# Between attention and experts: earlier stores, gathers ahead of expert numbers, second expert's weights loaded in advance

## The chip, the cores and the metric

The program runs on one core of a Trainium2 chip. The metric is the time of one execution on the device, in microseconds (us). A core has five engines that each work through their own instructions in order: TensorE (PE, with its weight loads listed apart as PEld), VectorE (DVE), ScalarE (ACT), GpSimd (POOL) and SyncE (SP). In this kernel SP issues nearly all plain DMAs, and POOL issues the indirect ones (gathers and scatters of rows by index). Engines wait for each other, and for DMAs, through semaphores.

## The reference

Attention over 2 x 576 rows with 8 heads, then a mixture of 8 experts with one expert per row, then a dense two-layer block. Cut to what matters:

```
x = attention(q, k, v)                  # rotary q and k; softmax; 1152 rows of 512
logits = normalised(x) @ normalised(expert_emb).T / tau
expert_idx = argmax(logits, axis=1)
for e in range(8):                      # w1[e]: 512 x 1024, w2[e]: 1024 x 512
    mask = expert_idx == e
    h = maximum(x[mask] @ w1[e], 0)
    out[mask] = gate_w[mask, None] * (h @ w2[e])
g = softplus(out @ w_in)                # 512 x 2048
result = g @ w_out                      # 2048 x 512
```

For the inputs that are timed, the reference sends 109, 200, 97, 486, 143, 31, 85 and 1 rows to the eight experts.

## The kernel before, in words

All matrix products are in float32, made of parts: each operand is split into a high part (a cast on ACT) and the rest (a subtraction on VectorE), and three products are added up. The program is written out in order by hand (`tc.manual_schedule()`): each engine gets its instructions in the order in which the Python code records them, and the tile framework adds the semaphore waits.

Three stages follow each other. **Attention** handles 16 heads in a loop over 72 steps; `xout` (L629 to L637) turns the output of a head into `xrow`, the rows of x, with one VectorE instruction per head (L637) and into `zp`, its share of the expert logits (L636). `x_store` (L170, L171) writes columns of `xrow` to `xs` in DRAM, where the rows can be gathered by expert. The columns of heads 8 to 13 (batch 1, `0:6*D`) are stored from inside the loop.

The **transition** decides which row goes where. `first_max` finds the expert of each row, `rank_mm`, `count_mm`, `places` and `at_places` number the rows within their experts by small matmuls, and `sequence` and `block_places` lay them out in blocks of at most 128 rows of one expert: at most 16 blocks, here 13. `idx[:, n]` holds the rows of block n, `eid[n]` its expert, `chg[n]` whether the expert differs from that of block n - 1. `gather(n)` (L963) fetches block n from `xs` into one of three buffers `xg`. PE runs `warm(WARM1)` (L676), 40 small matmuls whose results are not used.

The **expert stage** then goes through the blocks: `x_t` transposes the gathered rows (PE, L968), `x_ev` splits them (ACT L972, VectorE L973), `layer1` (L989), `relu` (L996), `h_t` and `h_ev` (again L968, L972, L973), `layer2` (L1018). Weights come in quarters of 512 KB: `fetch_w(n, l, c)` loads quarter c of layer l for block n into `raws_w[l, c]` (`raw00` to `raw03` for layer 1, `raw10` to `raw13` for layer 2), `split_hi` casts it on ACT (L950), `split_lo` subtracts on VectorE (L954) and then asks for the same quarter of the next block. For a block whose expert is that of the block before, the load is skipped by a condition in the DMA. Expert 0's first-layer weights are loaded and split during attention and lie elsewhere (`first_weights`), so that `raw00` to `raw03` are first written for block 1. A final stage does the dense block.

Around the change the order on SP is: the store of columns `0:6*D` (L170, L171), four loads of expert 0's second layer (L939), the store of the last two heads' columns (L170, L171), then, once `eid` can be read into registers (L943), the four loads of block 1's first layer (L945). Each SP DMA takes the next of eight completion semaphores in turn and waits until that semaphore's last DMA has landed; in the listings they are DMAHW0 to DMAHW7.

Of the kernel before, what the change touches and what calls it, by code (L numbers as in the profile page):

```python
# [20 lines left out]
ALU = mybir.AluOpType  # L21
# [74 lines left out]
def moe_kernel(ctx: ExitStack, tc: tile.TileContext, q, k, v, emb, tau, w1, w2, w_in, w_out, rope, tab, out):  # L96
# [182 lines left out]
    def sequence(cnt, q):  # L279

        used = w([P, E, E], "used")
        V.tensor_tensor(used, bc(cnt, E, 2), bc(tb("thr"), E, 1), op=ALU.is_gt)
        nov = q["nov"] = w([P, E], "nov")
        V.tensor_reduce(nov, used, axis=AX.X, op=ALU.add)
        yield
        V.tensor_tensor(used, tb("lt").rearrange("p (a b) -> p a b", a=E), bc(nov, E, 1), op=ALU.mult)
        st = q["st"] = w([P, E], "st")
        V.tensor_reduce(st, used, axis=AX.X, op=ALU.add)
        V.tensor_tensor(st, st, tb("ev"), op=ALU.add)
        be = q["be"] = w([P, NBLK, E], "be")  # L290
        V.tensor_tensor(be, bc(tb("n16"), E, 2), bc(st, NBLK, 1), op=ALU.is_ge)
        ef = w([P, NBLK], "ef")
        V.tensor_reduce(ef, be, axis=AX.X, op=ALU.add)
        V.tensor_scalar(eid, ef, -1.0, None, op0=ALU.add)
        V.tensor_tensor(chg[:, 1:NBLK], ef[:, 1:NBLK], ef[:, 0:NBLK - 1], op=ALU.not_equal)

    def block_places(q):
# [3 lines left out]
        V.tensor_tensor(total, nov[:, E - 1:E], st[:, E - 1:E], op=ALU.add)  # L301
        V.tensor_scalar(nblk, total, 1.0, None, op0=ALU.add)
        ok, at = (w([P, JB, E], n) for n in ("ok", "at"))
# [38 lines left out]
    with actx:  # L342
# [173 lines left out]
        heads, tiles = {}, {}  # L516
        late, rest = [], []

# [105 lines left out]
        def xout(i, left=None):  # L624
# [7 lines left out]
            def ev():  # L632
                ri = heads[i]['ri']
                V.reciprocal(ri, ri)
                ri = ri.unsqueeze(2)
                V.tensor_tensor(zp[b][:, :, h], px[:, :, D:D + E], ri.to_broadcast([P, 5, E]), op=ALU.mult)  # L636
                (rest if i == NH - 1 else late).append(lambda: V.tensor_tensor(xrow[b][:, :, h * D:h * D + D], px[:, :, 0:D], ri.to_broadcast([P, 5, D]), op=ALU.mult))  # L637

# [275 lines left out]
    if True:  # L914
# [15 lines left out]
        def fetch_w(n, l, c):  # L930

            if n >= NB:
                return
# [4 lines left out]
            if n == 0:  # L938
                SY.dma_start(raws_w[l, c], src[0, c])  # L939
                return  # L940
            always = n == 1 and l == 0
            if n not in regs:
                regs[n] = [SY.value_load(t[0:1, n:n + 1], min_val=0, max_val=m) for t, m in ((eid, E - 1), (chg, 1))]  # L943
            e, new = regs[n]
            SY.dma_start(raws_w[l, c], src[ds(e, 1), c].rearrange("e p f -> (e p) f"), **({} if always else dict(cond=new > 0)))  # L945

# [196 lines left out]

        for c in range(4):
            fetch_w(0, 1, c)
        pr1, pval, pcnt = bank(5), bank(JB), bank(1)[:, 0]
# [6 lines left out]
        for _ in first_max(1):  # L1153
            pass
        for r in rest:
            r()
        x_store(1, 6 * D, DM)
        rank_mm(1, pr1)
        count_mm(1, pcnt)
        for c in range(4):  # L1160
            split_hi((0, 1, c))
# [9 lines left out]
        gather(0)  # L1171
        V.tensor_copy(vals[0], pval)
        for _ in sgen:
            pass
        for c in range(4):
            fetch_w(1, 0, c)
        block_places(q)
        in_block(q, 1, 5)
        V.tensor_scalar(idx[:, 1:5], choose(q, vals[0], 1, 5)(), float(SKIP), None, op0=ALU.add)
        gather(1)  # L1180
        gg = [gate(b, gate_tmp) for b in range(B)]
        for _ in range(2):
            next(gg[0])
        split_lo((0, 1, 0))
        x_ev(0, x_t(0))
        for _ in layer1(0):
            pass
# [9 lines left out]
        for _ in range(4):  # L1197
            next(gg[0])
        for c in range(1, 4):
            split_lo((0, 1, c))  # L1200
        in_block(q, 5, NBLK)
# [254 lines left out]
```

## Time and profile before

| what | us |
|---|---|
| median of 3 runs (593.17 to 597.6) | 593.63 |
| profiled execution | 594.01 |
| its span, first to last instruction | 592.2 |
| PE busy | 549.3 |
| VectorE busy | 464.9 |
| ACT busy | 438.2 |

In a timeline a row gives start, duration, engine, line, operation, output and inputs, the number of merged instructions and, in brackets, how long the engine was idle before it and what ended that. A windows row gives, for a stretch, its length, then each engine's busy time with instructions in parentheses, then the clock that PE was granted as a share of 2.4 GHz (0.50 is 1.2 GHz), the mean busy share of the 16 DMA engines and what they moved. Names lose their buffer numbers in the profile: `raw` stands for all eight weight quarters.

### The profile page before, as it was taken

To read this page: it belongs to the slowest core of one execution; us is meant where nothing else is said; L and a number is where in the kernel's file an instruction comes from. 1 tells how busy PE (TensorE), PEld (TensorE's weight loads), DVE (VectorE), ACT (ScalarE), POOL (GpSimd) and SP (SyncE) were. 2 spreads that over 40 slices of the span, in tenths; PEclk is the share of its full clock that TensorE was granted. 3 is DMA by queue.
4 is the path that set the end of the run, shared out by engine and by line. 5 is a ranking of instruction groups with operands and counts; after the bars stand their busy time and mean duration, and the time that the engine had idled before them with its cause. 6 is when DMAs were issued, how large, how long until landed. Compare 5 with 4: busy or idle time off the path is not lost. (4 is left out here: it accounts for less than half of the span.)

```text
span 592.2 us, 9785 instructions
## 1 busy us (share of the span) xinstructions
PE 549.3 (93%) x3227; PEld 479.0 (81%) x3227; DVE 464.9 (79%) x775; ACT 438.2 (74%) x827; POOL 202.9 (34%) x305
## 2 busy tenths in 40 slices
PE   5699999999997789999999999969999999999995
PEld 4489999999986668787777888858888999888994
DVE  7998787879787499989999998776877766687233
ACT  3678878887875287599998898777877877767551
POOL 7999998569422330132222261200000000000033
PEclk9899999999998689999999999998999999999998
DMA  5423000061006635594348696262232222100012
GB/s 152 125 70 96 23 1 3 28 193 61 7 1 222 233 126 169 203 343 156 119 147 308 257 378 228 87 221 91 88 107 85 94 71 72 37 0 1 1 72 89
DMA packets 37270, 70.56 MB, mean 119 GB/s; under 512 B 8146, under 2 KB 23890, under 8 KB 37088
## 3 DMA queue, kind: packets, MB, share of 16 engines
q1 hardware_dynamic: 34272, 62.64, 31.8%
q0 software_dynamic: 2800, 7.09, 3.3%
q8 instruction: 27, 0.44, 0.3%
q10 hardware_dynamic: 144, 0.16, 0.2%
q14 instruction: 27, 0.22, 0.1%
HBM read 89.01 MB, written 8.13 MB: 164 GB/s over the span
## 5 line engine op out<-in xcount | busy, mean ns | idle before, releaser
L954 DVE TENSOR_TENSOR wt<-raw,wt 128x1024 fp32r<-128x1024 f32 x100 | 116.4, 1220 | 5.7 <-ACT wt L950 5.7
L1319 PE MATMUL ph<-yt,wt 128*128 128x320 f32 (+1 forms) x576 | 106.9, 340 | 4.2 <-ACT r__5678 L1331 3.4
L1319 PEld LDWEIGHTS ph<-yt,wt 128*128 128x128 f32 x576 | 95.1, 191 | 13.5 <-ACT r__5678 L1331 3.8
L1366 PE MATMUL po<-wt,g 128*128 128x512 f32 x432 | 104.0, 391 | 0.7 <-ACT g L1350 0.5
L950 ACT CAST wt<-raw 128x1024 fp32r<-128x1024 f32 x100 | 98.9, 1068 | 3.5 <-DMA raw<-in_moe_w_dram 1.9
L1366 PEld LDWEIGHTS po<-wt,g 128*128 128x128 f32 x432 | 80.2, 188 | 18.0 <-ACT g L1350 1.0
L1018 PE MATMUL py<-wt,ht 128*128 128x512 f32 x312 | 76.7, 397 | 3.3 <-DVE wt L954 2.6
L1383 POOL DMA_INDIRECT out_dram<-acc,otok x9 | 9.6, 1066 | 191.1 <-DVE acc L1380 190.5
L989 PE MATMUL ph<-wt,xt 128*128 128x512 f32 x288 | 71.0, 401 | 3.6 <-ACT hr L996 3.1
L1018 PEld LDWEIGHTS py<-wt,ht 128*128 128x128 f32 x312 | 57.5, 188 | 17.1 <-DVE wt L954 4.5
L989 PEld LDWEIGHTS ph<-wt,xt 128*128 128x128 f32 x288 | 54.2, 192 | 15.1 <-ACT hr L996 3.3
L562 ACT ACTIVATE p<-sc,nm 128x576 f32<-128x576 f32 x72 | 53.9, 749 | 15.4 <-DVE nm L556 15.4
L556 DVE TENSOR_REDUCE nm<-sc 128x1 f32<-128x576 f32 x72 | 54.1, 752 | 2.3 <-PE sc L552 1.3
L575 ACT CAST ph<-tp 128x512 fp32r<-128x512 f32 (+1 forms) x80 | 42.8, 546 | 14.8 <-PE tp L568 14.4
L552 PE MATMUL sc<-kt,qt 128*128 128x288 f32 x256 | 50.2, 318 | 2.1 <-ACT p L562 1.2
L586 DVE TENSOR_TENSOR pl<-tp,ph 128x512 fp32r<-128x512 f32 (+1 forms) x80 | 49.4, 627 | 0.0
L568 PE MATMUL tp<-idf,p 128*128 128x128 f32 x288 | 44.7, 278 | 4.8 <-DVE pl L586 3.5
L402 POOL TENSOR_TENSOR t<-qk,ropet 128x256 f32<-128x256 f32 x58 | 41.6, 745 | 10.9 <-DMA qk<-in_k_dram 10.5
L1351 DVE TENSOR_TENSOR g<-e,g 128x512 fp32r<-128x512 f32 (+2 forms) x33 | 24.3, 740 | 25.3 <-ACT g L1350 25.3
L1350 ACT CAST g<-e 128x512 fp32r<-128x512 f32 (+2 forms) x33 | 21.7, 659 | 30.3 <-PE po L1366 22.9
L613 PE MATMUL po<-ph,vs 128*128 128x288 f32 x128 | 36.5, 307 | 3.7 <-DVE kt L456 1.4
L568 PEld LDWEIGHTS tp<-idf,p 128*128 128x128 f32 x288 | 32.3, 144 | 9.0 <-issue 4.2
(246 smaller groups left out, 1023.2 us busy)
## 6 DMA issues: line engine op xcount, KB each, us to landing
raw<-in_moe_w_dram SPq DMA_DIRECT2D x112, 512.0 KB
raw<-in_moe_w_in_dram SPq DMA_DIRECT2D x16, 512.0 KB
raw<-in_moe_w_out_dram SPq DMA_DIRECT2D x16, 512.0 KB
yr<-ys SPq DMA_DIRECT2D x9, 256.5 KB
qk<-in_k_dram SPq DMA_DIRECT2D x8, 256.0 KB
qk<-in_q_dram SPq DMA_DIRECT2D x8, 256.0 KB
vv<-in_v_dram SPq DMA_DIRECT2D x8, 256.0 KB
xs<-xrow SPq DMA_DIRECT2D x1, 1024.0 KB
```

What stands on the lines that cost most here:

```text
L552: T.matmul(sc[:, n, 0:288], lhsT=w, rhs=r, start=(x == 0), stop=(x == len(mm) - 1))
L556: V.tensor_reduce(nm, tiles['sc', t][:, :, 0:288], axis=AX.XY, op=ALU.max, negate=True)
L562: A.activation(p.rearrange("p (n t) -> p n t", n=2), tiles.pop(('sc', t))[:, :, 0:288], AF.Exp, bias=tiles.pop(('nm', t)), accum_out=head( ...
L568: T.transpose(tp[:, x], p[:, x * P:x * P + P], idf)
L575: A.copy(columns(head(i))['ph'][:, :, c * P:c * P + w], tp[:, :, x * w:x * w + w])
L586: V.tensor_tensor(hd['pl'][:, :, sl], tp[:, :, x * w:x * w + w], f(hd['ph'][:, :, sl]), op=ALU.subtract)
L950: A.copy(wt[:, 0], raw)
L954: (eng or V).tensor_tensor(wt[:, 1], raw, f(wt[:, 0]), op=ALU.subtract)
L989: T.matmul(ph[i], lhsT=xt[:, a, c], rhs=wt[:, r, 512 * i:512 * i + 512] if n else wt[r][:, 512 * i:512 * i + 512], start=(c == 0 and a == ...
L1018: T.matmul(py, lhsT=ht[c // 2][:, a, k], rhs=rhs[:, s], start=(c == 0 and r == 0 and a == 0 and s == 0), stop=(c == 3 and r == 1 and a == 1))
L1319: T.matmul(phs[i][:, 0:n1 - n0], lhsT=wt[:, a, k], rhs=yts[p][:, r, k, n0:n1], start=(k == 0 and a == 0 and r == 0), stop=(k == 3 and a == 1))
L1366: T.matmul(outs[i][c], lhsT=g[:, a, c * P:c * P + P], rhs=wt[:, r], start=(first and a == 0 and r == 0), stop=(last and a == 1))
```

## The change

Five things are changed. The `xrow` instruction of the last head is issued at once rather than after `first_max`, and the store of the last two heads becomes two stores of one head each. Four loads of expert 1's first-layer weights are placed ahead of these stores on SP, with two of expert 0's four second-layer loads between; the other two follow the stores. For block 1, the loads that come after `eid` is known are carried out only where the expert is 0 (`e < 1`). The index column of block 1 is worked out by itself, ahead of `eid`, `chg` and `nblk`, and `gather(1)` follows it; columns 2 to 4 come later. And of expert 0's four second-layer quarters, two are cast where all four were, one is subtracted earlier, and the last two are cast and subtracted together after the squares that follow `relu(0)`.

```
 def sequence(cnt, q):
         V.tensor_tensor(st, st, tb("ev"), op=ALU.add)
+        yield
         be = q["be"] = w([P, NBLK, E], "be")
...
 def block_places(q):
-        V.tensor_scalar(nblk, total, 1.0, None, op0=ALU.add)
+        q["total"] = total
...
 def xout(i, left=None):
-                (rest if i == NH - 1 else late).append(lambda: V.tensor_tensor(xrow[b][:, :, h * D:h * D + D], px[:, :, 0:D], ri.to_broadcast([P, 5, D]), op=ALU.mult))
+                late.append(lambda: V.tensor_tensor(xrow[b][:, :, h * D:h * D + D], px[:, :, 0:D], ri.to_broadcast([P, 5, D]), op=ALU.mult))
...
 def fetch_w(n, l, c):
-            always = n == 1 and l == 0
+            second = n == 1 and l == 0
...
-            SY.dma_start(raws_w[l, c], src[ds(e, 1), c].rearrange("e p f -> (e p) f"), **({} if always else dict(cond=new > 0)))
+            SY.dma_start(raws_w[l, c], src[ds(e, 1), c].rearrange("e p f -> (e p) f"), cond=e < 1 if second else new > 0)
...
         for c in range(4):
+            SY.dma_start(raws_w[0, c], w1[1, P * c:P * c + P])
+        for c in range(2):
+            fetch_w(0, 1, c)
+        x_store(1, 6 * D, 7 * D)
+        x_store(1, 7 * D, DM)
+        for c in range(2, 4):
             fetch_w(0, 1, c)
...
-        for r in rest:
-            r()
-        x_store(1, 6 * D, DM)
         rank_mm(1, pr1)
         count_mm(1, pcnt)
-        for c in range(4):
+        for c in range(2):
             split_hi((0, 1, c))
...
         gather(0)
         V.tensor_copy(vals[0], pval)
+        next(sgen)
+        block_places(q)
+        in_block(q, 1, 2)
+        V.tensor_scalar(idx[:, 1:2], choose(q, vals[0], 1, 2)(), float(SKIP), None, op0=ALU.add)
+        gather(1)
         for _ in sgen:
             pass
+        V.tensor_scalar(nblk, q["total"], 1.0, None, op0=ALU.add)
         for c in range(4):
             fetch_w(1, 0, c)
-        block_places(q)
-        in_block(q, 1, 5)
-        V.tensor_scalar(idx[:, 1:5], choose(q, vals[0], 1, 5)(), float(SKIP), None, op0=ALU.add)
-        gather(1)
+        split_lo((0, 1, 0))
+        in_block(q, 2, 5)
+        V.tensor_scalar(idx[:, 2:5], choose(q, vals[0], 2, 5)(), float(SKIP), None, op0=ALU.add)
         gg = [gate(b, gate_tmp) for b in range(B)]
         for _ in range(2):
             next(gg[0])
-        split_lo((0, 1, 0))
         x_ev(0, x_t(0))
+        split_lo((0, 1, 1))
         for _ in layer1(0):
             pass
...
         for _ in range(4):
             next(gg[0])
-        for c in range(1, 4):
-            split_lo((0, 1, c))
+        for c in range(2, 4):
+            split_w(0, 1, c)
         in_block(q, 5, NBLK)
```

The order of PE's and POOL's instructions is the same in both programs. On three engines it is not. The first place is VectorE at the end of attention (`zs`, `z`, `m`, `eq`, `mx`, `oh`: steps of `first_max` for batch 1; `rk`: the first step of `places`). Before:

```order
L636 TENSOR_TENSOR zp_98<-px,rinv 128x5x8
L184 TENSOR_TENSOR z_2889<-zs_2785,zp_98 128x40
L187 TENSOR_REDUCE m_2891<-z_2889 128x5
...
L198 TENSOR_TENSOR oh_2898<-tabt,mx_2896 128x40
L637 TENSOR_TENSOR xrow_96<-px,rinv 128x5x64
L220 TENSOR_TENSOR rk_2921<-bank,oh_2898 128x40
```

The same place in the changed program:

```order
L637 TENSOR_TENSOR zp_98<-px,rinv 128x5x8
L638 TENSOR_TENSOR xrow_96<-px,rinv 128x5x64
L184 TENSOR_TENSOR z_2898<-zs_2785,zp_98 128x40
L187 TENSOR_REDUCE m_2900<-z_2898 128x5
...
L198 TENSOR_TENSOR oh_2907<-tabt,mx_2905 128x40
L220 TENSOR_TENSOR rk_2923<-bank,oh_2907 128x40
```

The last head's `xrow` has moved ahead of the six instructions of `first_max`.

The second place is SP from the store of columns `0:6*D` on, with the waits of each instruction (DMAHW: landings of earlier SP DMAs; DVE, Pool, PE: that engine's progress). Before:

```order
L170 DMA xs_105<-xrow1_96 512x1x384 [waits DVE_49]
L171 DMA xs_105<-xrow1_96 64x384 [waits DMAHW3_49]
L939 DMA raw10_2860<-in_moe_w2_dram 128x1024 [waits DMAHW5_49,DMAHW4_49]
L939 DMA raw11_2861<-in_moe_w2_dram 128x1024 [waits PE_49]
L939 DMA raw12_2862<-in_moe_w2_dram 128x1024
L939 DMA raw13_2863<-in_moe_w2_dram 128x1024 [waits DMAHW7_49]
L170 DMA xs_105<-xrow1_96 512x1x128 [waits DMAHW0_49,DVE_49]
L171 DMA xs_105<-xrow1_96 64x128 [waits DMAHW1_49]
L943 TENSOR_LOAD eid_111 [waits DVE_49]
...
L945 DMA raw00_2856<-in_moe_w1_dram 128x1024 [waits DMAHW2_49,Pool_49]
```

The changed program, after the same first two rows:

```order
L1147 DMA raw00_2857<-in_moe_w1_dram 128x1024 [waits DMAHW4_49,DMAHW7_49,DVE_49,Pool_49]
L1147 DMA raw01_2858<-in_moe_w1_dram 128x1024 [waits DMAHW5_49,DMAHW0_49]
L1147 DMA raw02_2859<-in_moe_w1_dram 128x1024 [waits DMAHW1_49]
L1147 DMA raw03_2860<-in_moe_w1_dram 128x1024
L941 DMA raw10_2861<-in_moe_w2_dram 128x1024
L941 DMA raw11_2862<-in_moe_w2_dram 128x1024 [waits PE_49]
L170 DMA xs_105<-xrow1_96 512x1x64 [waits DMAHW2_49]
L171 DMA xs_105<-xrow1_96 64x64 [waits DMAHW3_49]
L170 DMA xs_105<-xrow1_96 512x1x64 [waits DMAHW4_49]
L171 DMA xs_105<-xrow1_96 64x64 [waits DMAHW5_49]
L941 DMA raw12_2863<-in_moe_w2_dram 128x1024 [waits DMAHW6_49]
L941 DMA raw13_2864<-in_moe_w2_dram 128x1024 [waits DMAHW7_49]
```

Four loads that stood behind the last stores now stand ahead of them, and the first of the row waits for VectorE. In both programs `raw00` lies at bytes 61280 to 65376 of a partition, where attention's last `rinv` (bytes 63296 to 63316) lay before; the VectorE instruction that the wait counts up to is the `xrow` of the last head (L638), the last reader of that `rinv`.

The third place is ACT from the casts of expert 0's second layer to the first cast of `h_ev(0)` (raw_2856 to raw_2859 are `raw00` to `raw03`, raw_2862 and raw_2863 are `raw12` and `raw13`; in the changed program each number is one higher; `junk` rows are the squares of `gate`). Before:

```order
L950 CAST wt<-raw_2862 128x1024
L950 CAST wt<-raw_2863 128x1024
L250 ACTIVATE junk,n_3043<-xrow_95 128x512 x2
L972 CAST xt<-pt 128x512
...
L972 CAST xt<-pt 128x512
L950 CAST wt<-raw_2858 128x1024
L950 CAST wt<-raw_2859 128x1024
L996 ACTIVATE hr<-ph 128x512 x2
L250 ACTIVATE junk,n_3043<-xrow_95 128x512 x3
L972 CAST ht<-pt 128x512
```

The same place in the changed program:

```order
L250 ACTIVATE junk,n_3053<-xrow_95 128x512 x2
L974 CAST xt<-pt 128x512
...
L974 CAST xt<-pt 128x512
L952 CAST wt<-raw_2859 128x1024
L952 CAST wt<-raw_2860 128x1024
L998 ACTIVATE hr<-ph 128x512 x2
L250 ACTIVATE junk,n_3053<-xrow_95 128x512 x3
L952 CAST wt<-raw_2863 128x1024
L952 CAST wt<-raw_2864 128x1024
L974 CAST ht<-pt 128x512
```

Two casts have moved from ahead of the first squares to behind the three squares that follow `relu(0)`; VectorE's two subtractions that read them stay where they were, between those of `raw02` and `raw03` and the index work for columns 5 to 15 (L326).

## Rows read from the trace of the kernel before

**Rows 1.** The page: PE's granted clock in 40 slices (9: 90% or more).
```profile
PEclk9899999999998689999999999998999999999998
```

**Rows 2.** Windows, the transition in stretches (columns as said above).
```profile
178.00:180.00 2.00, 1.98 (x18) 1.83 (x18) 1.90 (x7) 1.12 (x4) 1.04 (x2) 1.00 0.00 0
180.00:182.50 2.50, 2.27 (x18) 1.89 (x16) 1.76 (x6) 1.06 (x2) 0.64 (x2) 1.00 1.01 332
182.50:186.50 4.00, 3.29 (x35) 2.83 (x35) 1.69 (x7) 1.49 (x3) 1.45 (x3) 1.00 0.97 300
186.50:189.00 2.50, 0.39 (x10) 0.29 (x9) 2.29 (x11) 1.95 (x3) 0.00 (x0) 0.99 0.94 380
189.00:190.50 1.50, 0.36 (x6) 0.46 (x7) 1.40 (x6) 0.50 (x1) 0.00 (x0) 0.50 0.68 191
190.50:191.75 1.25, 1.25 (x15) 1.25 (x13) 1.15 (x7) 0.94 (x1) 0.00 (x0) 0.50 0.10 23
191.75:194.50 2.75, 2.75 (x29) 2.75 (x27) 2.51 (x12) 1.45 (x5) 1.30 (x1) 0.50 0.00 0
```

**Rows 3.** Timeline of VectorE: end of attention to the first index column.
```profile
185.76 0.20 DVE L636 TENSOR_TENSOR zp<-px,rinv 128x40 f32<-128x40 f32 x1 [2.20 <-PE px L629]
...
187.28 0.48 DVE L637 TENSOR_TENSOR xrow<-px,rinv 128x320 f32<-128x320 f32 x1
...
190.64 0.16 DVE L1170 TENSOR_SCALAR idx<-bank 128x1 int32<-128x1 f32 x1
```

**Rows 4.** Timeline of SP (DMA issues), the same stretch.
```profile
178.79 0.58 SPq L170 DMA_DIRECT2D xs<-xrow  x1
180.15 2.79 SPq L939 DMA_DIRECT2D raw<-in_moe_w_dram  x4
187.79 0.54 SPq L170 DMA_DIRECT2D xs<-xrow  x1
```

**Rows 5.** Timelines of POOL and PE: gather(0), then blocks 0 and 1 on PE.
```profile
192.73 1.30 POOL L963 DMA_INDIRECT xg<-xs,idx  x1 [6.92 <-DVE nblk L302]
...
196.91 1.11 PE L968 MATMUL pt<-idf,xg 128*128 128x128 f32 x4 [2.05 <-DMA xg<-xs,idx]
...
209.81 4.42 PE L989 MATMUL ph<-wt,xt 128*128 128x512 f32 x12 [3.06 <-ACT hr L996]
...
214.93 3.01 PE L989 MATMUL ph<-wt,xt 128*128 128x512 f32 x12
```

**Rows 6.** DMA view of 187.8 to 189, then of 189 to 191.2: packets by size.
```profile
DMA packets 109, 0.41 MB, mean 338 GB/s; under 512 B 13, under 2 KB 13, under 8 KB 108
DMA packets 621, 0.32 MB, mean 143 GB/s; under 512 B 40, under 2 KB 616, under 8 KB 621
```

**Rows 7.** DMA view of 195.5 to 204.5: queue q1 is SP's (packets, MB, share).
```profile
q1 hardware_dynamic: 707, 2.60, 73.9%
```

**Rows 8.** Timelines of ACT, VectorE and PE around relu(0), up to block 0's layer 2.
```profile
207.27 1.99 ACT L950 CAST wt<-raw 128x1024 fp32r<-128x1024 f32 x2
...
212.19 0.18 ACT L250 ACTIVATION_READ_ACCUMULATOR junk<-xrow 128x1 f32 x1
208.35 5.77 DVE L954 TENSOR_TENSOR wt<-raw,wt 128x1024 fp32r<-128x1024 f32 x5 [0.25 <-ACT wt L950]
214.04 1.55 DVE L326 TENSOR_TENSOR inr<-at,tabt 128x792 bf16<-128x792 f32 x1
217.73 0.68 DVE L973 TENSOR_TENSOR ht<-pt,ht 128x512 fp32r<-128x512 f32 x1
217.78 2.58 PE L1018 MATMUL py<-wt,ht 128*128 128x512 f32 x9
218.47 2.14 PEld L1018 LDWEIGHTS py<-wt,ht 128*128 128x128 f32 x10 [0.50 <-DVE ht L973]
```

**Rows 9.** Windows, after the transition; then PE's waits from 220 to 385 (us, times, longest).
```profile
220.00:260.00 40.00, 38.62 (x194) 31.80 (x193) 35.97 (x55) 30.71 (x42) 6.87 (x12) 1.00 0.62 212
PE py L1018 <- DVE wt L954: 2.6, 5, 0.6
```

More of the change, by code (lines that the diff above doesn't have):

```diff
@@ L516, in moe_kernel @@
         heads, tiles = {}, {}
-        late, rest = [], []
+        late = []
         def head(i):
```

## The prediction, as put on record before the changed kernel ran

> **What bounds the kernel now.** I began with the page: PE is busy for 549.3 of 592.2 us, and its granted clock dips in slices 13 to 15, between 178 and 222 us [rows 1]. Everything that the change moves lies there, so I cut it into windows [rows 2]. The reader should see two things in them. PE, nearly always busy until 186.5, does 0.39 us of work between 186.5 and 189; from 189 on its clock is 0.50, the lower of its two levels (1.2 GHz), and what keeps it busy until 194.5 is the warm-up that feeds nothing. And the 16 DMA engines are full (0.94 to 1.01) from 180.0 to 189.0, then carry 191 GB/s, and are empty from 191.75: that burst is the store of `0:6*D`, four weight quarters and the last store.
>
> The timelines say what PE waits for. Its first useful matmuls, the transposes of block 0, begin at 196.91, on `gather(0)`, which POOL starts at 192.73 [rows 5]. The profile puts that wait down to `nblk`, which the gather doesn't read; the index column it does read was done at 190.80 [rows 3]. So it waited for the rows to be in DRAM: the last store, whose bytes end at about 190.5. The last store is thus what the transition ends on, and the question is when it lands in the changed program. After it PE has little slack: 38.6 of 40 us busy from 220 to 260, and its largest wait in all of 220 to 385 is 2.6 us [rows 9]. A late block 0 is passed on to the end.
>
> **Term 1: the store.** The last `xrow` moves ahead of six small instructions. `zp` ends at 185.96, the next instruction began at 186.00, and an `xrow` takes 0.48 [rows 3]: ready at 186.5 in place of 187.76. SP starts 0.03 later, as it did at 187.79 [rows 4]. That is 1.3 us won. The six instructions, and the index column with them, come 0.5 later: 191.3, still ahead of the store.
>
> But the stores now stand behind six weight loads on SP, and the first of these, `raw00`, waits for that same `xrow`, since it overwrites the last reader's `rinv`. So nothing of the burst but the first store can start at 180.15, as `raw10` to `raw13` did. SP's queue stands until 186.5; the engines run empty after the first store's bytes (to 182.5 [rows 2]). An issue at 178.79 had bytes moving from 180.0 [rows 2, 4], 1.2 us later, so the loads begin to move at 187.7. Six quarters are 6 x 0.524 = 3.15 MB; at 380 GB/s, the rate of the stretch that holds weights alone, 8.3 us: 196.0. Then the stores. They carry the same 0.295 MB, but cut by head: 1152 pieces of 256 bytes for 576 of 512. The old ones took 1.5 us from 189.0 to 190.5, at about half the rate of the weights, so pieces count there as well as bytes: 1.5 if bytes alone count, 3.0 if pieces alone do. I take the middle, 2.2. The last byte is then at 198.2 against 190.5: **+7.7 us**, between 7.0 and 8.5. Gather, transposes and the clock follow as before: the clock is at its low level by then in both programs.
>
> On small pieces the Trainium skill ("DMA: Bandwidth & Descriptors", section Specifications) states that transfers under 512 B are read, modified and written. By it the stores would take more than the 3.0 us, and the sum would be over 0.8 us higher; no row before the change shows a store of 256 bytes.
>
> That DMAs of one queue are served in order I read from the packets. The store was issued at 187.79; from 187.8 to 189.0 the engines still moved 96 packets of 2 to 8 KB and none between 512 B and 2 KB, and from 189.0 on 576 of the store and five large ones [rows 6].
>
> **Term 2: two casts moved to where there was room on ACT but not on VectorE.** The casts of `raw12` and `raw13` now follow the three squares behind `relu(0)`, which end at 212.37; two casts take 1.99 [rows 8], and ACT was idle there. VectorE is not: before, it went through five subtractions from 208.35 to 214.12, 1.15 each, then the index work for columns 5 to 15, 214.04 to 217.73, and only then the second half of `h_ev(0)`, which PE waited 0.50 us for at the start of `layer2(0)` [rows 8]. Now it does two subtractions (to 210.7), waits until the first cast ends at 213.4, and does the other two: the index work starts at 213.4 + 2 x 1.15 = 215.7, not 214.04. As PE was already waiting there, it loses the whole **+1.7 us**. The bounds are 0, if VectorE makes it good in its 4 us of slack between 220 and 260 and PE's 2.6 us of waits on it shrink [rows 9], and 1.7.
>
> **What costs nothing.** The loads in advance gain PE nothing: its 3.06 us wait at 209.81 is for `relu(0)` [rows 5], which stands on ACT behind two casts that themselves follow `x_ev(1)`; no row there waits for a weight. `gather(1)` is issued right behind `gather(0)`, but its rows are read only after `layer1(0)`. The subtraction of `raw11` fills VectorE's wait during `layer1(0)`; if that cover were gone it would cost 1.2. The four conditional loads of block 1 are skipped: between 195.5 and 204.5 SP's queue moved 2.60 MB [rows 7], five quarters, and the fifth of these is loaded only if block 1 has a new expert. They still wait on SP for the stores' semaphores, and a cast for them, but both are through by 201 and the cast of `raw00` comes after 205. The loads of `raw12` and `raw13` follow the stores, by about 201, and are needed after 220.
>
> **The sum.** 594.0 (profiled) + 7.7 + 1.7 = 603.4. The median before is 0.4 below the profiled run, so I predict **603.0**: slower by 1.6%. I count 1%, 5.9 us, as what a measurement of this kernel tells from no change; the border is 599.6.
>
> **Rivals.**
> *The clock falls once more.* In term 2 PE stands still for about 2.2 us (0.5 + 1.7). After the wait of 3.06 its next 12 matmuls took 4.42 us, where 12 later ones took 3.01 [rows 5]: 1.4 us. If the shorter stop does the same, 604.4. For it: the dip after a stop little longer; against it: after the 0.50 us stop nothing of the kind is seen. 12%.
> *The preload isn't held back.* If what `raw00` waits for is over by 180, the six loads follow the first store at 182.5, end at 190.8, the stores at 193.0: +2.5, and with term 2 the median is 597.8, within 1%. For it: before, `raw00` named no wait for VectorE; against it: it was issued long after, when that wait was met anyway. 6%.
> *The stores pass the loads.* If the engines take the small stores out of turn, the gather waits for its index alone: the column at 191.3 is up to 1.4 us ahead of 192.73, less what POOL needs to start; the gain is 0 to 1.4. With term 2 the median is 593.9 to 595.3; with term 2 absorbed, 592.2 to 593.6, faster than before but by less than 1%. The point that decides is whether the last store lands by 191.3. Against it: the order of packets [rows 6]. Also the last head's two stores must wait for `raw00` and `raw01` to land, whose bytes end at 187.7 + 2 x 1.4 = 190.5, so that the full gain is out of reach. 6%. The Trainium skill (the same page, section Queues, rings and completion order) has descriptors consumed in ring order while a later one may finish its write before an earlier one; by that a store could overtake the loads still in flight, and the packets here show no more than that.
> *The change doesn't skip the reload.* If block 1 belonged to expert 0, 2.1 MB would be read once more, 5.5 us at 380 GB/s, behind the stores and `raw12` and `raw13`: the last quarter would land near 207, ahead of its cast behind `x_ev(1)`, which 207.27 + 7.7 puts at 215 [rows 8]. It would cost nothing, and [rows 7] exclude it; it has no chance of its own.
>
> **Chances and range.** The sum as it stands, 76%; by its bounds it reaches from 600.6 (term 1 at 7.0, term 2 at 0) to 603.8 (8.5 and 1.7). The clock 12%, to 605.2 with the stores at their slowest. The last 12% (6 and 6) lie between 592 and 598. The range leaves out those 12% and little above: 598.5 to 606. Slower by over 1%: 0.84 (of the 88%, 4 for errors in both terms together); within 1%: 0.15; faster by over 1%: 0.01, which no case gives.
>
> **What would show each step.** In the changed profile `raw00`'s first load should be issued at about 186.5, not 180; DMA should be idle from 182.5 to 187.7 and full from there to 196; the last stores' bytes should end near 198, and the first gather start near 200.4 and the first transposes of block 0 near 204.6. Around relu(0) VectorE should wait some 2.7 us for a cast, and `layer2(0)` should wait about 2 us for `h_ev`. The prediction is wrong if loads move at 182.5, if packets of the stores appear among those of the first six loads, or if the time from the first transposes to the end of the span is shorter than before by more than a microsecond.

## The result, and the profile after

The changed kernel takes **602.36 us** (median of 4 runs, 600.94 to 604.63) against 593.4 of the kernel before beside it (4 runs): 1.0129 times, 95% interval 1.0094 to 1.0164. The forecast was 603.0. The profiled execution took 602.95 us with a span of 601.2, 9.0 more than before.

On the page of the changed kernel, PE's granted clock in 40 slices answers to [rows 1]: the dip sits in the same three slices and is deeper.

```profile
PEclk8899999999997589999999999998999999999998
```

The transition in windows (us, busy time by engine, PEclk, DMA share, GB/s) answers to [rows 2]:

```profile
180.00:182.50 2.50, 2.28 (x20) 2.04 (x19) 1.77 (x6) 1.19 (x3) 1.40 (x3) 1.00 0.70 252
182.50:187.50 5.00, 4.07 (x40) 3.43 (x39) 2.73 (x9) 0.80 (x2) 1.45 (x3) 1.00 0.18 54
187.50:189.00 1.50, 0.41 (x10) 0.32 (x9) 0.99 (x5) 0.00 (x0) 0.00 (x0) 0.65 0.41 63
189.00:195.00 6.00, 3.81 (x41) 3.92 (x42) 5.48 (x27) 0.00 (x0) 0.00 (x0) 0.52 1.00 406
196.75:198.10 1.35, 0.00 (x0) 0.00 (x0) 0.94 (x1) 0.87 (x2) 0.00 (x0) 1.00 1.22 312
198.10:203.90 5.80, 0.00 (x0) 0.00 (x0) 1.50 (x5) 1.90 (x5) 3.30 (x3) 0.51 0.90 324
```

The DMA engines, full from 180 to 189 before, now stand almost empty for five microseconds and are full from 189 on; PE, whose warm-up ends at 195.4, stands still for the 8.51 us before 203.94 (its first row below). VectorE's timeline gives the marks of [rows 3]:

```profile
186.53 0.20 DVE L637 TENSOR_TENSOR zp<-px,rinv 128x40 f32<-128x40 f32 x1 [2.18 <-PE px L630]
186.64 0.48 DVE L638 TENSOR_TENSOR xrow<-px,rinv 128x320 f32<-128x320 f32 x1
...
191.68 0.16 DVE L1175 TENSOR_SCALAR idx<-bank 128x1 int32<-128x1 f32 x1
```

SP's timeline (DMA issues) answers to [rows 4], and the list of SP's waits (us in total, times, longest) names the reason:

```profile
179.55 0.58 SPq L170 DMA_DIRECT2D xs<-xrow  x1
...
187.19 1.76 SPq L1147 DMA_DIRECT2D raw<-in_moe_w_dram  x4
...
192.00 1.98 SPq L171 DMA_DIRECT2D xs<-xrow  x1
```

```profile
SPq L1147 <- DVE xrow L638: 6.3, 1, 6.3
```

The early loads (L1147) stood 6.3 us at the head of SP's queue until the last `xrow` was done, then went out with the stores behind them. The DMA view from 196.75 to 198.1 shows the stores (pieces of 256 bytes; [rows 6] for the old ones), the one from 198.1 to 206 what SP's queue moved afterwards (as [rows 7]):

```profile
DMA packets 1255, 0.42 MB, mean 312 GB/s; under 512 B 1224, under 2 KB 1224, under 8 KB 1255
```

```profile
q1 hardware_dynamic: 419, 1.49, 48.4%
```

The 1.49 MB are nearly three quarters: `raw12`, `raw13` and one of the next block. Reloading block 1's four would have been 2.1 MB more; the conditional loads were skipped. The page of the changed kernel agrees: over the whole execution SP's queue moved 62.64 MB, as much as before.

```profile
q1 hardware_dynamic: 34880, 62.64, 31.9%
```

POOL's and PE's timelines answer to [rows 5] and the end of [rows 8]:

```profile
199.77 1.30 POOL L965 DMA_INDIRECT xg<-xs,idx  x1 [13.20 <-DVE idx L1190]
```

```profile
203.94 1.11 PE L970 MATMUL pt<-idf,xg 128*128 128x128 f32 x4 [8.51 <-DMA xg<-xs,idx]
205.73 8.62 PE L991 MATMUL ph<-part,xt 128*128 128x512 f32 x24 [0.68 <-ACT xt L974]
...
217.85 4.61 PE L991 MATMUL ph<-wt,xt 128*128 128x512 f32 x12 [3.06 <-ACT hr L998]
...
226.02 0.61 PE L1020 MATMUL py<-wt,ht 128*128 128x512 f32 x2
228.03 2.56 PE L1020 MATMUL py<-wt,ht 128*128 128x512 f32 x10 [1.40 <-DVE ht L975]
230.44 0.60 PE L970 MATMUL pt<-idf,xg 128*128 128x128 f32 x4
```

VectorE in the same stretch, which answers to the rest of [rows 8]:

```profile
221.37 2.88 DVE L956 TENSOR_TENSOR wt<-raw,wt 128x1024 fp32r<-128x1024 f32 x2 [2.62 <-ACT wt L952]
224.18 0.97 DVE L327 TENSOR_TENSOR inr<-at,tabt 128x792 bf16<-128x792 f32 x1
...
227.29 0.68 DVE L975 TENSOR_TENSOR ht<-pt,ht 128x512 fp32r<-128x512 f32 x1
```

**A ruler.** The end of attention is not at the same time in every profile: `zp` began at 185.76 before, at 186.53 here, and anywhere from 185.89 to 188.57 in the profiles below. So positions are counted from the start of `zp`. Two of them are enough: when `gather(0)` starts, and when PE begins the transposes of block 2 (220.88 before, 230.44 after). From there to the end of the span it is 371.3 us before and 370.8 after, so the damage is all ahead of that point. The 9.0 us of the two spans split like this (differences of rows of before and of after):

| stretch | before | after | more |
|---|---|---|---|
| start of the span to `zp` | 185.76 | 186.53 | 0.77 |
| `zp` to `gather(0)` | 6.97 | 13.24 | 6.27 |
| `gather(0)` to block 0's transposes | 4.18 | 4.17 | 0.0 |
| from there to block 1's transposes (`layer1(0)` between) | 9.24 | 10.25 | 1.01 |
| from there to `layer2(0)` | 11.63 | 11.83 | 0.20 |
| `layer2(0)` to block 2's transposes | 3.10 | 4.42 | 1.32 |
| from there to the end of the span | 371.32 | 370.76 | -0.56 |

### The profile page after: what moved, and what is told of

It is laid out like the page before. It is cut to its first block, busy times and chain, and to the rows that moved or that the text cites. A ratio compares the mean times of both kernels' runs of the same rounds, so it can differ in the third digit from the quotient of the medians.

```text
span 601.2 us, 9800 instructions
## 1 busy us (share of the span) xinstructions
PE 552.0 (92%) x3227; PEld 481.8 (80%) x3227; DVE 464.1 (77%) x779; ACT 437.4 (73%) x827; POOL 203.7 (34%) x305
## 3 DMA queue, kind: packets, MB, share of 16 engines
q1 hardware_dynamic: 34880, 62.64, 31.9%
## 5 line engine op out<-in xcount | busy, mean ns | idle before, releaser
L553 PE MATMUL sc<-kt,qt 128*128 128x288 f32 x256 | 52.1, 327 | 1.5 <-ACT p L563 0.8
L553 PEld LDWEIGHTS sc<-kt,qt 128*128 128x128 f32 x256 | 38.2, 199 | 2.7 <-ACT p L563 1.3
```

Of the source, the lines that this page charges most:

```text
L553: T.matmul(sc[:, n, 0:288], lhsT=w, rhs=r, start=(x == 0), stop=(x == len(mm) - 1))
```

## Experiments

The theory was that of the prediction: `raw00`'s wait holds the whole queue (term 1), and two casts on ACT make VectorE late (term 2). The rivals were that the early bytes cost by themselves, or the small pieces, or the clock. A table at the end of this section has all runs; ratios are to the kernel before on the same chip, where it took 593.4 to 595.2 us, so rows are compared by their ratios.

### Without the preload

The changed kernel, with block 1's first-layer weights loaded as before and all else as changed.

```
-        for c in range(4):
-            SY.dma_start(raws_w[0, c], w1[1, P * c:P * c + P])
...
-  cond=e < 1 if second else new > 0)
+  **({} if second else dict(cond=new > 0)))
```

> The changed kernel without the four first-layer loads in advance (block 1's first-layer weights are loaded as in the kernel before, without a condition); the split stores, the early gather(1), the moved index work and the moved casts stay. Theory: the preload is term 1 and what is left is term 2: SP holds two quarters, the stores go out right behind the last xrow, gather(0) waits for its index alone, zp + 6.2 as in the run with split loads; 593.4 - 0.5 + 1.6 = 594.5, at most 595. Rival: the stores by head or the early gather(1) have their own price, and it stays over 597.

Measured: 593.78 us, 1.0009 times before (0.9983 to 1.0036). The preload is what the change loses. Timelines of this kernel, of SP, POOL and PE:

```profile
186.52 0.53 SPq L170 DMA_DIRECT2D xs<-xrow  x1
```

```profile
192.08 1.35 POOL L965 DMA_INDIRECT xg<-xs,idx  x1 [6.15 <-DVE st L289]
```

```profile
218.22 2.58 PE L1020 MATMUL py<-wt,ht 128*128 128x512 f32 x10 [1.61 <-DVE ht L975]
```

With only two quarters ahead of it the last store goes out as its row is done, and the gather starts at `zp` + 6.19. Term 2 is still there, as 1.61 us before `layer2(0)`; the 0.8 us won at the gather about pay for it.

### Nothing to wait for

The changed kernel with `rinv` in another pool, so that `raw00` overwrites nothing that the last head reads.

```
-  small.tile([P, 5], F32, tag="rinv", name="rinv")
+  rt.tile([P, 5], F32, tag="rinv", name="rinv", bufs=8)
```

> The changed kernel with rinv in another pool, so that raw00 no longer overwrites it and the first of the early loads need not wait for the last xrow. My theory: the six loads follow the first store without a gap, the stores end some 1.5 to 2.5 us later than before the change, and with the two later casts the time is 596.5 to 598 us. Rival (the six loads ahead of the stores cost the whole amount by themselves and the idle queue costs nothing): about 602 us.

Measured: 598.72 us, 1.0095 (1.0062 to 1.0127). SP's waits and POOL's timeline:

```profile
SPq L1147 <- POOL rinv L591: 0.6, 1, 0.6
```

```profile
197.58 1.69 POOL L965 DMA_INDIRECT xg<-xs,idx  x1 [9.21 <-DVE nblk L1185]
```

```profile
186.00:194.00 8.00, 3.97 (x55) 3.73 (x54) 5.05 (x25) 0.40 (x1) 1.45 (x3) 0.92 1.01 373
```

The 6.3 us on SP are 0.6, and the gather starts 4.0 us earlier, at `zp` + 9.26. The rest of the delay goes with the bytes: six quarters in place of four still lie ahead of the last stores, and the DMA engines are full (1.01) up to 194. This is the prediction's rival of a preload that isn't held back (597.8), built on purpose, and it is still some 5 us slower than before. It came out 0.7 above the upper end that I gave it.

### The stores ahead of the loads

```
+        x_store(1, 6 * D, 7 * D)
+        x_store(1, 7 * D, DM)
         for c in range(4):
             SY.dma_start(raws_w[0, c], w1[1, P * c:P * c + P])
```

> The changed kernel with the two stores of the last heads ahead of the six weight loads on SP; nothing else differs. My theory (the first gather waits for stores that stand behind six loads): the last store is issued at the last xrow and its bytes are through about 2 us later, so gather(0) waits for its index column alone and block 0's transposes begin some 7 to 8 us earlier than in the changed kernel. Not all of that reaches the end: raw10 and raw11 still come after four other loads, some 8 us behind the last xrow, and ACT has their casts and two squares ahead of x_ev(0), so that x_ev(0) ends up some 2 us later than before the change. With the 1.7 us of the two later casts: about 597 us. Rival (it is the 2 MB of early loads as such that cost, wherever the stores stand): about 602 us.

Measured: 600.14 us, 1.0106 (1.007 to 1.0142): less than half of what I expected to win. POOL, PE and ACT, and a windows row of the gather:

```profile
193.00 1.34 POOL L965 DMA_INDIRECT xg<-xs,idx  x1 [6.16 <-DVE st L289]
```

```profile
199.69 1.11 PE L970 MATMUL pt<-idf,xg 128*128 128x128 f32 x4 [3.94 <-DMA xg<-xs,idx]
202.85 8.56 PE L991 MATMUL ph<-part,xt 128*128 128x512 f32 x24 [2.04 <-ACT xt L974]
```

```profile
199.90 1.04 ACT L952 CAST wt<-raw 128x1024 fp32r<-128x1024 f32 x1 [1.03 <-DMA raw<-in_moe_w_dram]
...
202.23 0.57 ACT L974 CAST xt<-pt 128x512 fp32r<-128x512 f32 x1
```

```profile
196.00:199.70 3.70, 0.01 (x1) 0.01 (x1) 0.79 (x1) 1.04 (x1) 0.34 (x1) 0.85 1.03 409
```

The gather starts at `zp` + 6.21, as early as without the preload (6.19). But its own bytes now share the DMA engines, full until the rows are there (1.03), with the six quarters: 6.7 us from its start to the transposes, where it was 4.2 before. And `x_ev(0)`'s cast stands on ACT behind the cast of `raw11`, which waits for its load until 199.90: PE waits 2.04 us for it, where it waits 0.68 in the changed kernel. I had counted on the late casts, not on the slow gather; moved out of the stores' way, the loads are in the way of what comes next.

### One store of 512-byte pieces for two of 256

```
-        x_store(1, 6 * D, 7 * D)
-        x_store(1, 7 * D, DM)
+        x_store(1, 6 * D, DM)
```

> The changed kernel with the last two heads stored by one call (576 pieces of 512 bytes) in place of two calls (1152 of 256). Theory: the pieces cost by their bytes: in the changed kernel 1152 pieces moved in some 1.25 us, so one store saves nothing to 0.3 us: 602.1 to 602.4, and the gather starts at the same distance from the end of the loads' bytes. Rival: a piece under 512 bytes costs double; then the stores take half as long and the time falls by about 1.2 us, to 601.2.

Measured: 603.66 us, 1.0158 (1.0112 to 1.0205), and the gather at `zp` + 13.03 (13.24 with two stores). The DMA view of the stretch in which its store moved (198.4 to 199.75, 1.35 us again):

```profile
DMA packets 659, 0.50 MB, mean 370 GB/s; under 512 B 42, under 2 KB 608, under 8 KB 659
```

Half as many pieces, and the same stretch of time, in which the engines moved 370 GB/s for 312, with more of the weights among them. The gather comes 0.2 us earlier: about that much is what the small pieces cost here, too little to be told in the time of the kernel.

### The casts

In the changed kernel the casts of `raw12` and `raw13` were put ahead of the three squares; in the kernel before they were put behind them, with one subtraction earlier, as in the change.

```
-  for c in range(4):              # kernel before: all four casts in the transition
+  for c in range(2):
       split_hi((0, 1, c))
...
   x_ev(0, x_t(0))
+  split_lo((0, 1, 1))
...
-  for c in range(1, 4):           # behind relu(0) and three squares
-      split_lo((0, 1, c))
+  for c in range(2, 4):
+      split_w(0, 1, c)
```

> The kernel before with one part of the change alone: two of the four second-layer quarters of expert 0 are cast after the squares behind relu(0), and one subtraction comes earlier. My theory: 1.7 us slower than before, about 595.1 us. Rival (VectorE makes it good): 593.4 us, no change.

> The changed kernel with the casts of raw12 and raw13 ahead of the three squares behind relu(0) in place of after them. My theory: VectorE's wait of 2.6 us for the first of these casts goes, layer2(0) waits for h_ev(0) as it did before the change, and 1.7 us are won: about 600.6 us. Rival (VectorE makes the delay good later on, so that it never reached the end): 602.4 us.

The kernel before with the casts behind: 594.95 us, 1.0031 (1.0003 to 1.006). The changed kernel with them ahead: 602.86, 1.0167 (1.0135 to 1.02), which is not told apart from 1.0129. `layer2(0)` on PE, of the one and of the other:

```profile
220.59 2.56 PE L1018 MATMUL py<-wt,ht 128*128 128x512 f32 x10 [1.61 <-DVE ht L973]
```

```profile
227.20 2.89 PE L1020 MATMUL py<-wt,ht 128*128 128x512 f32 x12
```

The wait comes with the casts (1.61; 0.50 before) and goes with them (twelve matmuls in one piece). From `layer2(0)` to block 2's transposes it is 4.63 us with the casts behind, here and without the preload, against 3.10 before: +1.5. By the total the first run agrees and the second doesn't show it. The profile to set beside the second is that of the run with one store, whose gather starts at `zp` + 13.03 as well:

```profile
217.73 5.49 PE L991 MATMUL ph<-wt,xt 128*128 128x512 f32 x12 [3.06 <-ACT hr L998]
...
227.91 2.60 PE L1020 MATMUL py<-wt,ht 128*128 128x512 f32 x10 [0.33 <-DVE ht L975]
```

VectorE waits 2.63 us for the casts there, as in the changed kernel. But PE, with 5.49 us (granted clock 0.50 from 217 to 223) for the twelve matmuls that took 4.61 in the changed kernel, comes to `layer2(0)` late itself (226.97 for 226.02, with VectorE's `ht` at 227.17 for 227.29) and waits only 0.33 us. The stretch to block 2's transposes is 3.37 us, and 3.31 in the run with nothing to wait for; with the casts ahead it is 2.72. So the casts cost 1.3 to 1.5 us where PE comes in time, and 0.2 to 0.7 us where its own low clock makes it late.

### The clock

The changed kernel with more warm-up matmuls, so that PE is busy until the rows come.

```
-WARM0, WARM1 = 28, 40
+WARM0, WARM1 = 28, 180
```

> The changed kernel with 180 warm-up matmuls behind the transition in place of 40, so that TensorE does not stand still from 195.4 until block 0's rows are there at 203.9. Theory: of what the change costs, some 2.5 us are the clock, which in the changed kernel falls to 0.50 at 198.6, 3 us into that stop, and stays low for the whole of layer1(0) (24 matmuls 8.62 us, transposes 1.11). At full clock 24 of them take 24 x 3.01/12 = 6.0 us and the transposes half of 1.11: about 602.4 - 2.6 - 0.5 = 599.3, with layer1(0) near 6.0 us. Rival: layer1(0) is paced by what follows it (casts, the relu), so that the time stays at 602 though the clock is high.

Measured: 600.94 us, 1.013 (1.0082 to 1.0178): no gain that can be told. PE:

```profile
205.87 6.13 PE L991 MATMUL ph<-part,xt 128*128 128x512 f32 x24 [0.68 <-ACT xt L974]
...
215.50 3.06 PE L991 MATMUL ph<-wt,xt 128*128 128x512 f32 x12 [3.06 <-ACT hr L998]
...
225.68 2.56 PE L1020 MATMUL py<-wt,ht 128*128 128x512 f32 x10 [2.95 <-DVE ht L975]
```

At the higher level (granted clock 1.00 from 194 on) the two groups are 2.5 and 1.55 us shorter than in the changed kernel, and the wait for VectorE's `ht` is 1.55 longer: with a slow PE, VectorE's lateness was partly hidden. Counted from `zp` block 2's transposes come 2.2 us earlier; the ratio to the kernel before did not move (1.013 and 1.0129).

### Looking for a faster version

The sound part of the change alone on the kernel before: the last `xrow` behind `zp`, its store behind two of the four quarters.

```
-                (rest if i == NH - 1 else late).append(...)
+                late.append(...)
...
-        for c in range(4):
+        for c in range(2):
+            fetch_w(0, 1, c)
+        x_store(1, 6 * D, DM)
+        for c in range(2, 4):
             fetch_w(0, 1, c)
```

> The kernel before with the sound part of the change alone: the last xrow right behind zp, its store issued behind two of the four second-layer quarters in place of all four, no first-layer weights in advance. Theory: SP's queue holds only two quarters, so the store goes out as soon as xrow is done (1.3 us earlier than before) and lands ahead of the index column; the gather then waits for the column alone, which comes 0.5 us later than before: gather(0) 0 to 0.5 us earlier, 592.9 to 593.4. Rival: as in the changed kernel whatever stands ahead on SP holds the store, and the gather starts later than in the kernel before: over 594.

593.89 us, 0.9998 (0.9969 to 1.0026). Its gather starts at `zp` + 6.20 and the kernel before's at 6.97, 6.94, 6.73 and 6.02 in four profiles that keep its order (two with edits only behind the gather, one with the casts): the gain is between -0.2 and 0.8 us, and the time shows none.

Next, the wait of 3.06 us that no preload could shorten, by putting `relu(0)` first:

```
-        x_ev(1, x_t(1), "ht1")
+        x1 = x_t(1)
+        relu(0)
+        x_ev(1, x1, "ht1")
         gather(2)
         for c in range(2, 4):
             split_w(1, 0, c)
-        relu(0)
```

> The kernel before with relu(0) ahead of x_ev(1) and its neighbours on ScalarE. The prediction said that the 3.06 us wait at 209.81 is for relu(0), which stands behind two casts, and that weights in advance can't shorten it. Theory: relu(0) then starts at about 206.3 and ends at 207.4, x_ev(1) at 208.6 on VectorE, so layer1(1) starts 1.2 to 1.5 us earlier and the time is about 592.0. Rival: another wait on ScalarE or VectorE takes its place (the casts of block 1's weights, late by relu's 1.1 us), and the time stays at 593.4.

595.56 us, 1.0014 (0.998 to 1.0048). PE:

```profile
207.08 3.29 PE L989 MATMUL ph<-wt,xt 128*128 128x512 f32 x12 [0.73 <-ACT xt L972]
...
218.14 4.09 PE L1018 MATMUL py<-wt,ht 128*128 128x512 f32 x10 [3.60 <-DVE ht L973]
```

The 3.06 are 0.73, and a wait of 3.60 for VectorE takes their place. So VectorE's index work for columns 5 to 15, needed only by `gather(5)`, went behind `h_ev(0)`:

```
-        in_block(q, 5, NBLK)          # and pick, idx, pgen
...
         h_ev(0, pts, ...)
+        in_block(q, 5, NBLK)          # and pick, idx, pgen
```

> The kernel before with relu(0) ahead of x_ev(1), as in the run that gained nothing, and with VectorE's index work for columns 5 to 15 (3.6 us) moved behind h_ev(0). Theory: in the earlier run layer1(1) did start earlier and the time came back as a 3.60 us wait of layer2(0) for h_ev(0) on VectorE; without the index work ahead of it that wait is 0 to 0.5 us, so the time is 3 us less than there: 590 to 591. Rival: VectorE is what bounds this stretch as a whole, and the index work is only paid two instructions later (casts of block 2): 593 to 594.

593.3 us, 0.9983 (0.9952 to 1.0014). The 3.60 us are 0.48, and 0.90 appear at the start of `layer1(2)`, for `x_ev(2)` on VectorE: the gain on PE brings VectorE's next debt forward. In the time of the kernel the rival was right. In the rows, block 2's transposes come 3.6 us earlier after `zp` than before; 1.3 us of that are given back behind them (372.61 us to the end), and attention ended 2.0 us later in this profile. Then all three edits together, with more warm-ups:

```
-WARM0, WARM1 = 28, 40
+WARM0, WARM1 = 28, 56
```

> The kernel before with what held: relu(0) first and the index work later, the last xrow behind zp and its store behind two of the four second-layer quarters, and 56 warm-ups for 40. Theory: the gains add where they lie on different stretches: first gather 0 to 1.0 us earlier, layer1(0) up to 1.3 us faster at full clock, 3 us from VectorE: 588.5 to 590. Rival: a faster layer1(0) is given back as a longer wait for VectorE, as with 180 warm-ups in the changed kernel: 590 to 591, or no better than without.

**591.77 us, 0.9969 (0.9945 to 0.9994)**: faster than the change, and by 0.3% than the kernel before, though less than the 588.5 to 590 expected. It is the best of five variants, and its interval only just leaves out 1. PE:

```profile
199.57 6.13 PE L989 MATMUL ph<-part,xt 128*128 128x512 f32 x24 [0.67 <-ACT xt L972]
...
223.55 5.28 PE L989 MATMUL ph<-wt,xt 128*128 128x512 f32 x22 [0.90 <-DVE xt L973]
```

Block 2's transposes come 29.37 us after `zp` (35.12 before), 5.7 earlier, and the median fell by 1.7. Of the difference 0.8 is given back behind that point (372.15 us to the end, 371.32 before); in this profile attention also ended 2.7 us later than in the profile of before, and how much of that belongs to this kernel one profile can't tell.

The last try moved the index work once more, behind `x_ev(2)` and block 2's casts:

```
         for c in range(2, 4):
             split_w(2, 0, c)
+        in_block(q, 5, NBLK)          # and pick, idx, pgen
         for _ in l2:
             pass
```

> The last kernel with all three edits, with the index work for columns 5 to 15 (3.1 us of VectorE) moved once more, from behind h_ev(0) to behind x_ev(2) and block 2's casts. Theory: there it held back the second half of x_ev(2), for which TensorE waited 0.90 us at the start of layer1(2); that wait goes, and the time falls by 0.9 us, to 590.9. Rival: VectorE has no slack left here: the wait comes back at the next thing that it owes TensorE (h_ev(1), behind the same work), and the time stays at 591.8.

593.53 us, 0.9976 (0.9948 to 1.0003), which the ratio does not tell apart from 0.9969. The gain of 0.9 us did not come, as the rival had it; PE shows why:

```profile
227.68 5.53 PE L1018 MATMUL py<-wt,ht 128*128 128x512 f32 x23 [1.30 <-DVE wt L954]
...
240.72 2.38 PE L277 MATMUL bank<-ogs,row 128*128 128x72 f32 x10 [2.73 <-DVE less L313]
242.84 5.00 PE L989 MATMUL ph<-wt,xt 128*128 128x512 f32 x12
```

The 0.90 are gone; 1.30 and 2.73 us of waits on VectorE come later, and behind the second the next twelve matmuls take 5.00 us in place of 3.01. From block 2's transposes to the end of the span it is 376.0 us (372.15 without this edit).

| kernel | median us | ratio | `zp` starts | `gather(0)` after `zp` | block 2's transposes after `zp` |
|---|---|---|---|---|---|
| before | 593.4 | | 185.76 | 6.97 | 35.12 |
| the change | 602.36 | 1.0129 | 186.53 | 13.24 | 43.91 |
| no preload | 593.78 | 1.0009 | 185.89 | 6.19 | 34.74 |
| nothing to wait for | 598.72 | 1.0095 | 188.32 | 9.26 | 38.34 |
| stores first | 600.14 | 1.0106 | 186.79 | 6.21 | 40.74 |
| one store | 603.66 | 1.0158 | 188.24 | 13.03 | 42.10 |
| change, casts ahead | 602.86 | 1.0167 | 188.49 | 13.03 | 41.43 |
| before, casts behind | 594.95 | 1.0031 | 188.57 | 6.02 | 34.43 |
| change, 180 warm-ups | 600.94 | 1.013 | 186.36 | 13.64 | 41.73 |
| before, early store | 593.89 | 0.9998 | 188.14 | 6.20 | 33.14 |
| relu first | 595.56 | 1.0014 | 186.42 | 6.94 | 35.62 |
| and index later | 593.3 | 0.9983 | 187.79 | 6.73 | 31.50 |
| all three, 56 warm-ups | 591.77 | 0.9969 | 188.48 | 6.20 | 29.37 |
| index last | 593.53 | 0.9976 | 186.21 | 6.20 | 29.68 |

## Why the prediction was right

- **Term 1, +7.7: right in its mechanism, 1.4 too large.** The loads went out at `zp` + 0.66 (I said 0.78), after a wait of 6.3 us for `xrow` alone; DMA carried 54 GB/s from 182.5 to 187.5. Counted from `zp`, their bytes end where I put them (10.2). Two terms behind were too large: the stores took no more than 1.35 us, not 2.2; and from their end to the gather it was 1.7, not the 2.2 of before. I had read a price of pieces out of the old store's half rate, but the engines were only 0.68 busy then [rows 2]; behind the loads they were full, and moved 312 GB/s with pieces of 256 bytes, 370 with pieces of 512. The rule of the Trainium skill ("DMA: Bandwidth & Descriptors", section Specifications) that transfers under 512 B are read, modified and written, by which the stores would have taken more than 3.0 us, shows little of a price here: 1224 packets under 512 B fit into 1.35 us, and with larger pieces the gather came 0.2 us earlier.
- **"Gather, transposes and the clock follow as before"** is the step that failed. Gather and transposes did. The clock did not: it had come back to 1.00 by the end of the warm-up, PE then stood still, and from 198.1 to 203.9 it is 0.51. It stays low until 211 to 212, where before the change it rose between 202 and 203 (windows before, then after):

```profile
202.00:203.00 1.00, 1.00 (x5) 0.81 (x4) 0.03 (x1) 0.00 (x0) 0.00 (x0) 0.71 0.99 385
204.00:212.00 8.00, 7.33 (x19) 5.58 (x20) 4.09 (x4) 2.48 (x3) 1.00 (x1) 0.51 0.39 117
```

  `layer1(0)` took 8.62 us, all but its last two to three microseconds at the lower level (1.2 GHz), where it took 7.6 before: +1.0. Which group of matmuls pays differs between profiles (`layer1(0)` took 7.17 us with one store, and the next twelve 5.49). From block 0's transposes to `layer2(0)` it is 22.1 us in the change, 21.7 to 21.8 with one store, with the casts ahead and with nothing to wait for, 20.9 before and 20.3 without the preload: behind the preload's longer stop this stretch costs 0.8 to 1.2 us more than before.
- **Term 2, +1.7: right in its mechanism**, 1.3 here and 1.5 in two other kernels. VectorE waited 2.62 us for the casts (2.7 forecast) and finished two subtractions at 224.2; the index step behind them then took 0.97 us in place of 1.55, which I had taken over from before. That PE loses all of it holds only where PE comes in time: in the two profiles in which its own clock made it late, 0.2 to 0.3 us were left (3.31 and 3.37 for 3.10). The 2.6 us of [rows 9], with which I argued for the lower bound, is the sum of five waits, the longest of them 0.6.
- The errors partly cancel: 6.27 + 1.01 + 1.32 and 0.2 elsewhere make 8.8, against 9.4 forecast. That the total is closer than its parts is luck.
- **What costs nothing** held. The wait for `relu(0)` is 3.06 us to the hundredth with the weights there in advance, and 0.73 once `relu(0)` is moved: it never was a wait for weights. The reload was skipped.
- **The rivals.** The clock did fall, though not where I put it: behind the 1.40 us stop no group is slower; it was low behind the stop of 8.51 us, over `layer1(0)`, and with PE kept busy there it stayed at 1.00 (180 warm-ups). The preload that isn't held back gives 598.7, where I had 597.8. For the stores that pass the loads, the nearest case is the run with the stores first; even that is slower than before, since the loads then delay the gather and ACT.
- On [rows 5] I read the wait for the last store as what the transition ends on. With the same order the gather started at `zp` + 6.02 in one profile, 1.0 us behind its index column, as it does where the store goes out early: store and index end within a microsecond of each other, and which is last changes from run to run.

## What to carry to other kernels

A load in advance is only as early as the buffer that it overwrites: look up whose last reader that is, since on an in-order issue queue everything written behind it waits too, here 6.3 us for the store on which the next stage hangs. And before loading early, find a row in which somebody waits for that load: here there was none, and the wait beside it named ACT's order. When a wait on PE disappears, ask what VectorE or ACT owe it next; the saved time can reappear there, as 3.60 us did here for 3.06.

## What the runs showed of the hardware

Attention is the same code in all these kernels, yet its end moves by 2.8 us from profile to profile. One thing that differs is the speed of its first score matmuls: those of the kernel before, of the one with the casts behind, and of the one with the index last (attention's end at 185.76, 188.57 and 186.21):

```profile
10.30 1.19 PE L552 MATMUL sc<-kt,qt 128*128 128x288 f32 x7 [0.33 <-DVE qt L463]
```

```profile
10.71 2.77 PE L552 MATMUL sc<-kt,qt 128*128 128x288 f32 x8 [0.47 <-ACT qt L462]
```

```profile
10.15 2.77 PE L552 MATMUL sc<-kt,qt 128*128 128x288 f32 x8 [0.47 <-ACT qt L462]
```

Seven take 1.19 us in the first, eight 2.77 in the two others, twice as long each, though the record shows a granted clock of 1.00 from 10 to 14 us in all three. But it does not set the end of attention: the third, as slow at its start as the second, ends 2.4 us earlier. What sets either is open. It means that effects of 1 to 2 us are read from the ruler or from many runs, not from two spans; and the ruler too moves with the clock, as the casts show.
